# First feed-forward product of half batches 2.1, 3.0 and 3.1 in groups of four by seven block products

## The chip, the cores and the metric

The kernel runs on one core of one Trainium2 chip. The metric is device time in microseconds (us) of one execution, the median of several. A core has TensorE (PE in the profile, with its weight loads as PEld), VectorE (DVE), ScalarE (ACT), GpSimd (Pool) and SyncE (SP), each with its own queue of instructions that it works through in order; an instruction waits until what it reads has been written and what it overwrites has been read. Data lie in SBUF, and PE writes its products into PSUM.

## The reference

Attention in which a query sees only the keys of its own cluster, followed by a feed-forward layer:

```python
q_assign = np.argmax(np.einsum('bhsd,hcd->bhsc', q_n, c_n), axis=-1)
k_assign = np.argmax(np.einsum('bhsd,hcd->bhsc', k_n, c_n), axis=-1)
mask = q_assign[:, :, :, None] == k_assign[:, :, None, :]
scores = np.where(mask, scale * np.matmul(q, k.transpose(0, 1, 3, 2)), -1000000000.0)
attn = softmax(scores);  attn_out = np.matmul(attn, v)
...
x = attn_out.transpose(0, 2, 1, 3).reshape(B * S, H * D)
h = x @ w_in
g = h * (1.0 / (1.0 + np.exp(-h)))
out = g @ w_out
```

There are 4 batches, 8 heads, 768 positions of 64 features and 16 clusters. x is 3072 x 512, w_in 512 x 2048, w_out 2048 x 512; all arrays are float32, and the kernel multiplies in 16 bits (f16).

## The kernel before, in words

**Attention.** Each of the 32 pairs of batch and head is a job. Its q and k rows are normalised, split and transposed into a 128-row operand `ab`, whose lower rows are codes of the cluster, so that one product gives masked scores. A word `s.N` (L344) makes two score matmuls of 384 columns into PSUM, `x.N` (L349) is the exp on ACT that turns them into `P` (a pool of 14 buffers), `pv` (L361, 36 matmuls of 65 columns) multiplies by v with a column of ones, `nm` (L371 and L373 on DVE) divides by that column's sum, and `xd`/`xp` transpose the result into `xts[b, c]`, the operand x of the feed-forward layer. Code rows come about by `L` and `ls` (L179 on DVE), `mx` (L195), `ge` (L204), `sc` (L211 and L212 on Pool), `cx` (L220, a transposing DMA on SP) and `mv` (L224, a DMA from Pool or SP). `vc` (L285) is a cast of v on Pool.

**First product.** A half batch b.c (c is 0 or 1) has 384 tokens. Its hidden features are 16 blocks of 128. A unit `au.b.c.f` (L409) makes one block: four matmuls, one for each 128 rows of w_in, of 384 columns. The silu is kept as tanh and gating: with the weights halved beforehand, `t.b.c.f` (L429, ACT) takes the tanh out of PSUM, and `g.b.c.f` (L432, DVE) computes (tanh + 1) times h, with the tanh from SBUF and h from PSUM, into `gt`. A double unit `a2` makes two blocks in one pair of banks, with one tanh (L454) and one gate (L455) of 768 columns. A half batch so takes 64 matmuls of 384 columns.

**Second product.** For batch 0 it is plain (`b`, L467). From batch 1 on, `Pair` takes 128-token pieces two at a time by seven block products in place of eight: `ps` are sums of gated activations on DVE (L535, 128x1024 in f16), `pp` is a product of eight matmuls of 256 columns (L554), and `p1`, `pa`, `pu`, `pc`, `pd` put the results together on ACT and DVE (L560 to L586); `pf` and `pe` store them. `tw` (L500) are sums of w_out.

**Order.** All of this is one list of words, `order`, from L685 on; the program goes through it once, and each engine's queue holds its instructions in the order of the words. Attention of later batches is interleaved with the feed-forward layer of earlier ones, so that PE has work while ACT takes the exps. The words of the last third begin with score word `s.152`; at that place the attention of the last jobs (24 to 31), the rest of batch 2's first product and the second product of batches 1 and 2 lie beside each other.

Of the kernel before, what the change touches and what calls it, by code (L numbers as in the profile page):

```python
# [34 lines left out]
def kernel(  # L35
# [33 lines left out]
    def bank(name, dtype=f32, n=None):  # L69
        return ps.tile([128, 512 if dtype is f32 else 1024], dtype, name=name, tag=f"b{n}", bufs=1)  # L70
# [388 lines left out]

    pos = {}  # L460
# [217 lines left out]
    def stk_ev(pst1):  # L678
# [11 lines left out]
        hi.6.A hi.x0.P mx.4 L.3.16@1 v.6.S ge.4 ev.7.q.A lo.6 v.7.S cd.4 x.1 s.2 L.5.16@2 ce.4.D x.2 ev.7.k.D  # L690
        od.0 cg.4 s.3 tr.6.kq@03 mx.3 x.3 hi.x1.P ld.8 ge.3 s.4 ev.6.k.D x.4 ev.6.q.D s.5 mx.5 L.6.16@1 ge.5 x.5
        s.6 mx.6 cd.5 w.3 ct.3@03 x.6 ge.6 lo.x0 cd.6 vc.2 s.7 cq.3 s.8 w.0 x.7 ce.5.D tr.x0.k@0 ck.3 vc.5 cg.5
        L.7.32@2 ce.6.A vc.3 ls.7 pv.0.0.0.x@3 x.8 cg.6 s.9 vc.6 mx.7 tr.x0.q@1 x.9 w.1 ge.7 s.10 ev.x0.q.D cd.7
        vc.7 pv.0.0.1.x x.10 ev.x0.k.D s.11 w.2 lo.x1 pv.0.0.2.x ce.7.A w.5 L.x0.32.0.6@1 x.11 L.x0.32.6.12 cg.7
        s.12 w.9 ls.x0 w.7 pv.2.0.0.x@0 x.12 s.13 mx.x0 w.6 pv.2.0.1.x x.13 ge.x0 w.4 pv.2.0.2.x nm.0.0 cd.x0
        s.14 w.8 ce.x0.A tr.x1.k@2 x.14 s.15 cg.x0 ev.x1.k.D x.15 s.16 tr.x1.q@3 x.16 L.x1.32.0.6@1 s.17
        ev.x1.q.D x.17 L.x1.32.6.12 s.18 ls.x1 pv.4.0.0.x@2 x.18 nm.2.0 s.19 pv.4.0.1.x x.19 mx.x1 s.20 xp.2.0@3
        pv.4.0.2.x ge.x1 x.20 xe.2.0.D xp.0.0@0 s.21 nm.4.0 s.22 x.21 pv.6.0.y.0@3 xe.0.0.D x.22 xp.4.0@2 s.23
        xe.4.0.D ab.0.0.7@0 hi.8.D x.23 w.10.22 cd.x1 s.24 pv.6.0.y.1 x.24 w.11.23 s.25 nm.6.0 ab.0.0.6@2 x.25
        s.26 ce.x1.D xp.6.0@3 x.26 cg.x1 s.27 xe.6.0.D ab.0.0.0@1 ld.9 x.27 ae.0.0.7 ae.0.0.0 ae.0.0.6  # L700
        ab.0.0.4@3 t.0.0.0 ld.10 t.0.0.7 ae.0.0.4 g.0.0.0 s.28 t.0.0.6 s.29 g.0.0.7 x.28 ab.0.0.1@1 g.0.0.6
        ae.0.0.1 x.29 ab.0.0.2@0 ae.0.0.2 s.30 t.0.0.1 s.31 t.0.0.2 g.0.0.1 ab.0.0.3@2 t.0.0.4 ae.0.0.3
        ab.0.0.5@1 g.0.0.4 t.0.0.3 g.0.0.2 ae.0.0.5 au.0.0.8@3 t.0.0.5 g.0.0.3 x.30 au.0.0.10@0 g.0.0.5 t.0.0.8
        au.0.0.9@2 g.0.0.8 au.0.0.11@1 t.0.0.9 t.0.0.10 s.32 g.0.0.9 x.31 pv.0.1@3 g.0.0.10 hi.9.D t.0.0.11 s.33
        x.32 g.0.0.11 au.0.0.12@2 nm.0.1 x.33 au.0.0.13@0 lo.9 t.0.0.12 s.34 t.0.0.13 s.35 g.0.0.12 x.34
        au.0.0.14@1 tp.9 lo.8 xp.0.1@3 b.0.0.1.0@2 xe.0.1.A g.0.0.13 x.35 b.0.0.0.0@3 t.0.0.14 ld.11 s.36
        g.0.0.14 pv.2.1@0 x.36 hi.10.D tp.8 lo.10 s.37 au.0.0.15@1 b.0.0.0.1 t.0.0.15 x.37 v.8.S g.0.0.15 s.38
        ld.12 nm.2.1 b.0.0.0.2 x.38 v.9.S s.39 hi.11.A b.0.0.1.1 tp.10 x.39 lo.11 b.0.0.1.2 vc.8 s.40 L.9.32@1
        x.40 s.41 tp.11 L.8.32@0 x.41 b.0.0.0.3 ls.8 vc.9 mx.8 pv.4.1@0 be.0.0.0.A ls.9 mx.9 xp.2.1@3 s.42 ge.8
        s.43 xe.2.1.D x.42 v.10.S ge.9 cd.8@1 b.0.0.2.0@3 ce.8.D v.11.S x.43 hi.12.D cg.8 s.44 nm.4.1 b.0.0.2.1  # L710
        ld.13 x.44 lo.12 s.45 cd.9@1 xp.4.1@0 b.0.0.2.2 ce.9.D tp.12 xe.4.1.A x.45 L.10.32@1 s.46 ls.10
        L.11.32@0 x.46 s.47 ls.11 b.0.0.1.3 cg.9 x.47 mx.10 ld.14 ge.10 s.48 mx.11 s.49 x.48 cd.10@1 pv.6.1@0
        ge.11 v.12.S hi.13.D ce.10.A v.13.S x.49 cg.10 b.0.0.2.3 nm.6.1 be.0.0.1.A s.50 lo.13 bs.0.0.1 cd.11@1
        L.12.32@0 ce.11.A xp.6.1@2 s.51 ls.12 tp.13 xe.6.1.A au.0.1.1@1 be.0.0.2.D x.50 au.0.1.0@0 mx.12 x.51
        s.52 au.0.1.3@2 t.0.1.0 vc.13 t.0.1.1 g.0.1.0 ld.15 au.0.1.2@3 x.52 vc.10 ge.12 g.0.1.1 s.53 vc.11
        t.0.1.2 cg.11 au.0.1.5@0 hi.14.D t.0.1.3 od.1 ld.16 g.0.1.2 x.53 au.0.1.4@1 od.2 lo.14 vc.12 s.54 v.14.S
        t.0.1.4 pv.8.0@3 t.0.1.5 x.54 g.0.1.4 tp.14 s.55 g.0.1.5 cd.12@1 g.0.1.3 ce.12.A L.13.32@0 x.55 s.56
        ls.13 au.0.1.6@1 mx.13 au.0.1.7@2 cg.12 t.0.1.6 nm.8.0 vc.14 bs.0.0.2 au.0.1.8@0 t.0.1.7 g.0.1.6 v.15.S
        au.0.1.9@3 g.0.1.7 t.0.1.8 v.16.S ge.13 au.0.1.11@1 hi.15.D t.0.1.9 x.56 ld.17 au.0.1.10@2 g.0.1.9
        g.0.1.8 s.57 t.0.1.10 cd.13@3 s.58 x.57 ce.13.D au.0.1.12@0 g.0.1.10 cg.13 t.0.1.11 au.0.1.15@3 lo.15  # L720
        t.0.1.12 v.17.S x.58 au.0.1.13@2 vc.15 g.0.1.12 tp.15 s.59 g.0.1.11 t.0.1.13 L.14.32@0 x.59 s.60 ls.14
        au.0.1.14@1 mx.14 b.0.1.0.0@0 t.0.1.14 ge.14 v.18.S t.0.1.15 g.0.1.14 s.61 v.19.S hi.16.A g.0.1.15
        b.0.1.0.1 ld.18 g.0.1.13 x.60 cd.14@1 pv.10.0@3 v.20.S x.61 ce.14.A b.0.1.1.0@2 nm.10.0 cg.14 vc.19 s.62
# [220 lines left out]
```

## Time and profile before

| | us |
|---|---|
| median of three runs | 297.63 (297.48 to 298.21) |
| the profiled execution's span, first to last instruction | 295.4 |
| PE busy | 287.9 (97%) |
| DVE busy | 217.7 (74%) |
| ACT busy | 227.5 (77%) |
| Pool busy | 58.3 (20%) |
| first matmul of s.152 | 202.43 |
| exps, L349, 192 of them | 149.9 |
| first product, L409, 512 matmuls of 384 columns | 95.5 |
| gates of single units, L432, 110 of them | 57.8 |

The profile is of one execution; its span leaves out what lies before the first and behind the last instruction, and the difference to the median is 2.2 us. A row of the timeline gives the start in us from the span's start, the busy time in us, engine, line of the program, operation, output and inputs by the program's names, shape and count, and in brackets how long the engine stood idle before it and on what. Instructions on PE are pipelined, so that the busy times of neighbours overlap; what one costs is the distance from its start to the next one's. In the windows each engine has its busy time with the number of instructions, and the columns behind are TensorE's granted clock, the share of DMA and GB/s.

### The profile page before, as it was taken

What the parts mean: (1) busy time and instruction counts of PE and PEld (TensorE: products, weight loads), DVE (VectorE), ACT (ScalarE), POOL (GpSimd) and SP (SyncE); (2) the same over time, 40 slices, a digit from 0 to 9 for tenths busy, and PEclk for the clock granted to TensorE, in tenths of its full rate; (3) what the DMA queues carried; (4) which work ended last, traced back from release to release, by engine and by line L of the source; (5) the groups of instructions that cost most, each with busy time, mean ns of one, the idle gap of its engine ahead of it and who ended that gap; (6) DMA issues with size and microseconds to landing.
All of it is one profiled execution on the core that took longest, in us unless ns stands there. A gap on an engine that the chain in (4) does not pass through costs nothing.

```text
span 295.4 us, 8176 instructions
## 1 busy us (share of the span) xinstructions
PE 287.9 (97%) x3297; PEld 206.3 (70%) x3297; DVE 217.7 (74%) x458; ACT 227.5 (77%) x376; POOL 58.3 (20%) x116
## 2 busy tenths in 40 slices
PE   7799999999999999999999999999999999999995
PEld 3677666567666566678777778676777777777784
DVE  5899648677897998999578779957544563568582
ACT  4999999767987779898898988878688787464321
POOL 2489310020311102233401202542000000000000
PEclk9999999999999999999999999999999999999999
DMA  6978999998999979898689699984320210211023
GB/s 206 298 213 123 178 214 200 218 213 206 244 215 251 175 166 248 171 192 182 151 158 256 138 171 253 154 147 128 88 75 3 45 46 2 54 57 60 2 107 107
DMA packets 80548, 45.13 MB, mean 153 GB/s; under 512 B 58368, under 2 KB 77120, under 8 KB 80512
## 3 DMA queue, kind: packets, MB, share of 16 engines
q1 hardware_dynamic: 76080, 38.39, 57.2%
q0 software_dynamic: 4000, 5.82, 11.0%
q8 instruction: 25, 0.41, 0.6%
q10 hardware_dynamic: 432, 0.43, 0.4%
q14 instruction: 11, 0.09, 0.1%
HBM read 27.30 MB, written 6.29 MB: 114 GB/s over the span
## 4 chain that ended last, share of the span: by engine, by line
PE 89%; DMA 6%; DVE 3%; ACT 1%; SPq 0%; issue 0%; ACTq 0%
PE ph L409 28%; PE pS L344 19%; PE po L554 19%; PE pO L361 11%; PE po L467 7%; PE psN L167 3%; DMA ab<-cd 3%; DMA vn<-in_v_dram 2%; DMA raw<-in_q_dram 1%; DVE hl L120 1%; DVE ab L154 1%; PE junk L622 0%; DVE om L204 0%; DVE mxn L195 0%; PE px L382 0%; PE pTk L143 0%
## 5 line engine op out<-in xcount | busy, mean ns | idle before, releaser
L349 ACT ACTIVATE P<-pS 128x768 f16<-128x768 f32 x192 | 149.9, 815 | 22.8 <-PE pS L344 21.2
L409 PE MATMUL ph<-xt,win_s 128*128 128x384 f16 x512 | 95.5, 326 | 0.0
L344 PE MATMUL pS<-ab 128*128 128x384 f16 x384 | 86.0, 326 | 0.5 <-ACT P L349 0.2
L432 DVE SCALAR_TENSOR_TENSOR gt<-tn,ph 128x384 f16<-128x384 f32 x110 | 57.8, 550 | 35.9 <-ACT tn L429 35.5
L409 PEld LDWEIGHTS <-win_s 128*128 128x128 f16 x512 | 49.3, 98 | 30.2
L429 ACT ACTIVATE tn<-ph 128x384 f32<-128x384 f32 x110 | 51.0, 497 | 14.2 <-PE ph L409 13.3
L344 PEld LDWEIGHTS <-ab 128*128 128x128 f16 x384 | 34.4, 98 | 18.0 <-issue 0.9
L361 PEld LDWEIGHTS <-P 128*128 128x128 f16 x1152 | 39.8, 97 | 4.3 <-DVE ab L269 0.3
L361 PE MATMUL pO<-vt,P 128*128 128x65 f16 x1152 | 41.3, 193 | 0.2 <-DVE ab L269 0.2
L285 POOL CAST vt<-vn 128x384 f16<-128x384 f32 x32 | 18.7, 599 | 91.6 <-DMA vn<-in_v_dram 73.0
L554 PEld LDWEIGHTS <-gt 128*128 128x128 f16 x328 | 31.7, 98 | 6.6 <-DVE gt L535 0.2
L120 DVE SCALAR_TENSOR_TENSOR hl<-raw,hl 128x768 f16<-128x768 f32 (+3 forms) x35 | 31.8, 916 | 2.0 <-ACT hl L111 1.8
L554 PE MATMUL po<-wout_s,gt 128*128 128x256 f16 x216 | 28.0, 273 | 0.0
L467 PE MATMUL po<-wout_s,gt 128*128 128x512 f16 x96 | 24.0, 379 | 0.0
L167 PEld LDWEIGHTS <-ab 128*128 128x128 f16 x458 | 16.9, 97 | 3.9 <-DVE ab L154 0.8
L373 DVE TENSOR_TENSOR xn<-pO,zr 128x384 f16<-128x384 f32 x32 | 17.8, 558 | 1.1
L167 PE MATMUL psN<-stk,ab 128*128 128x32 f16 (+1 forms) x458 | 18.5, 188 | 0.2 <-DVE ab L154 0.2
L179 DVE TENSOR_REDUCE L<-psN 128x192 f32<-128x384 f32 (+1 forms) x27 | 14.9, 552 | 5.0 <-PE psN L167 4.7
L211 POOL TENSOR_SCALAR od<-od 128x96 f16<-128x96 f16 x16 | 8.0, 499 | 50.4 <-DVE od L204 50.4
L554 PE MATMUL po<-tw,sg 128*128 128x256 f16 x144 | 17.5, 273 | 0.0
L554 PEld LDWEIGHTS <-sg 128*128 128x128 f16 x144 | 14.1, 98 | 2.5
L467 PEld LDWEIGHTS <-gt 128*128 128x128 f16 x96 | 8.9, 98 | 8.2
(101 smaller groups left out, 252.1 us busy)
## 6 DMA issues: line engine op xcount, KB each, us to landing
raw<-in_k_dram SPq DMA_DIRECT2D x31, 192.0 KB, 3.8
out_dram<-ot SPq DMA_DIRECT2D x23, 256.0 KB, 2.5
vn<-in_v_dram SPq DMA_DIRECT2D x27, 192.0 KB, 3.7
raw<-in_q_dram SPq DMA_DIRECT2D x24, 192.0 KB, 3.4
win_s<-in_moe_w_in_dram POOLq DMA_DIRECT2D x8, 256.0 KB, 7.1
wout_s<-in_moe_w_out_dram POOLq DMA_DIRECT2D x4, 512.0 KB, 13.8
cp<-gt SPq DMA_DIRECT2D x4, 256.0 KB, 3.2
vn<-in_v_dram POOLq DMA_DIRECT2D x5, 192.0 KB, 3.6
```

The lines of the kernel that those rows point to most:

```text
L120: nc.vector.scalar_tensor_tensor(out=hl[:, s, 1, :], in0=raws[job.name][:, s, :], scalar=QS, in1=hl[:, s, 0, :], op0=ALU.mult, op1=ALU.sub ...
L167: nc.tensor.matmul(L[:, n % g, :, n // g], ab[:, i, :], stk[:, job.groups[i // 3][0], x : x + w], start=(x == 0), stop=(x + w == 2 * HC),)
L285: nc.gpsimd.tensor_copy(vt[:, :, 0:D], vns.pop(i))
L344: nc.tensor.matmul(pS[:, e, 0:HALF], abs_[kj.name][:, kn, :], rhs, start=True, stop=True)
L349: nc.scalar.activation(out=P, in_=pst.pop(u)[:, :, 0:HALF], func=AF.Exp, bias=0.0, scale=ESC)
L361: nc.tensor.matmul(o[:, (2 * t + h) * VW : (2 * t + h + 1) * VW], Ps[i + h, c, j // 2][:, j % 2, ts(t, 128)], vtb[(i + h) % 13][:, j, 0:VW ...
L373: nc.vector.tensor_tensor(out=xn, in0=ov[:, :, 0:D], in1=zr.unsqueeze(2).to_broadcast([128, 2 * NM, D]), op=ALU.mult)
L409: nc.tensor.matmul(ph[:, 0:HALF], win_s[:, r, ts(fb, 128)], xts[b, c][:, r, :], start=(r == 0), stop=(r == NR - 1))
L429: nc.scalar.activation(out=tn, in_=ph[:, 0:HALF], func=AF.Tanh, bias=0.0, scale=1.0)
L432: nc.vector.scalar_tensor_tensor(out=gt[:, fb, :], in0=tn, scalar=1.0, in1=ph[:, 0:HALF], op0=ALU.add, op1=ALU.mult)
L467: nc.tensor.matmul(po, gts[b, c][:, fc, ts(t, 128)], wout_s[:, fc, :], start=(fc == 0), stop=(fc == NFB - 1))
L554: nc.tensor.matmul(o, l[:, f, :], x, start=(f == 0 and k in begins), stop=(f == HK - 1), skip_group_check=True)
```

## The change

For half batches 2.1, 3.0 and 3.1 (48 of 128 feature blocks in all) the units are replaced by groups. A group `q.b.c.s`, s from 0 to 3, makes four feature blocks, 2s and 2s+1 of the lower eight and of the upper eight, for all 384 tokens. It sees w_in's part as 2 x 2 blocks (rows 0 to 255 and 256 to 511; lower and upper features) and x as 2 x 2 blocks (the same rows; tokens 0 to 191 and 192 to 383), and forms the product by seven block products in place of eight. A block product `q.b.c.s.k` is four matmuls of 192 columns (L539), so a group has 28 of them where units had 16 matmuls of 384.

The block products need sums: `un.n.s` (L482) are sums of w_in, `ws`, 128x512 in f16, 16 in all, which all three half batches use; `tt.b.c.n` (L494) are sums of x, 128x384, four for each half batch. Of the 16 sums of w_in 12 go to Pool and 4 to DVE, of the 12 of x 9 to Pool and 3 to DVE. Behind the products, three results of a group are copied out of PSUM into `cc` in float32 (`qc`, 24 on ACT, L549, and 12 on DVE, L551), and three sums on DVE (`qa`, L556) add a PSUM bank to a `cc`. Four tanh (`qt`, L563) and four gates (`qg`, L576) of 384 columns follow; for three of the four quarters h lies in `cc`, in SBUF, for the fourth in PSUM. `cc` comes from the same pool of 14 buffers as `P`. The nine double units of these half batches are gone with the single ones.

The list is another one from `s.152` on, the exps and scores of the last jobs come in another order among themselves, and unit au.2.0.14 stands behind s.152. The loads and stores on SP change places a little. The lines of the second product move by 121 (L535 is L656 after).

On Pool, from the last `mv.27` (L224 with ab_3682) on, the old order has, with `od` the code rows, `vt` the cast v and `uu` a zeroed buffer:

```order
L211 TENSOR_SCALAR od_508<-od_508 128x2x16x3
L212 TENSOR_SCALAR od_508<-od_508 128x2x16x3
L285 CAST vt3_73<-vn_4188 128x6x64
L504 MEMSET uu_4400 128x256
L224 DMA ab_3973<-cdt_4354 16x6x256
L285 CAST vt5_75<-vn_4599 128x6x64
```

and the new one, with `ws` the sums of w_in and `tt` those of x:

```order
L482 TENSOR_TENSOR ws_4348<-win_s_66 128x512
L482 TENSOR_TENSOR ws_4348<-ws_4348,win_s_66 128x512
L482 TENSOR_TENSOR ws_4393<-win_s_66,ws_4348 128x512
L482 TENSOR_TENSOR ws_4348<-win_s_66 128x512
L482 TENSOR_TENSOR ws_4393<-win_s_66 128x512
L211 TENSOR_SCALAR od_508<-od_508 128x2x16x3
L212 TENSOR_SCALAR od_508<-od_508 128x2x16x3
L494 TENSOR_TENSOR tt_4440<-xt_4009 128x384
L224 DMA ab_3973<-cdt_4406 16x6x256
L482 TENSOR_TENSOR ws_4476<-win_s_66,ws_4393 128x512
L494 TENSOR_TENSOR tt_4440<-xt_4009,tt_4346 128x384
L482 TENSOR_TENSOR ws_4476<-win_s_66 128x512
```

Five sums of w_in now stand ahead of the code rows of the last job but one, and more sums around the DMA that carries them.

On DVE, from the reduction `L` of the code rows beside s.152 on, the old order has:

```order
L179 TENSOR_REDUCE L_4345<-psN_4321 128x192
L195 TENSOR_REDUCE mxn_4356<-L_4345 128x12
L204 TENSOR_TENSOR od_508<-L_4345,mxn_4356 128x2x96
L432 SCALAR_TENSOR_TENSOR gt_3641<-tn_4343,ph_4338 128x384
L432 SCALAR_TENSOR_TENSOR gt_3641<-tn_4270,ph_4265 128x384
L432 SCALAR_TENSOR_TENSOR gt_3641<-tn_4365,ph_4360 128x384
L535 TENSOR_TENSOR sg_4402<-gt_3641 128x1024
L535 TENSOR_TENSOR sg_4414<-sg_4402,gt_3641 128x1024
```

The new one, up to the first sum `sg` for the second product:

```order
L494 TENSOR_TENSOR tt_4346<-xt_4009,tt_4346 128x384
L556 TENSOR_TENSOR cc_4383<-qb_4395,cc_4383 128x384
L551 COPY cc_4417<-qb_4412 128x384
L551 COPY cc_4424<-qa_4419 128x384
L482 TENSOR_TENSOR ws_4393<-ws_4393,win_s_66 128x512
L556 TENSOR_TENSOR cc_4424<-qb_4442,cc_4424 128x384
L556 TENSOR_TENSOR cc_4432<-qb_4412,cc_4432 128x384
L576 SCALAR_TENSOR_TENSOR gt_4377<-tn_4409,cc_4383 128x2x192
L656 TENSOR_TENSOR sg_4469<-gt_3641 128x1024
L482 TENSOR_TENSOR ws_4476<-win_s_66 128x512
L656 TENSOR_TENSOR sg_4491<-sg_4469,gt_3641 128x1024
```

What is shown here stands behind the same three gates; the two sums `sg` were next behind them, and now seven copies, sums and a gate stand in between, and a weight sum between the two.

The diff, cut to its core:

```diff
+    def w_sum(n, s, eng):
...
+        o = wsums[n, s] = hosts[tag][:, at]
...
+        x, y, op = {
+            1: (a21, a22, ALU.add), 2: (wsums.get((1, s)), a11, ALU.subtract),
+            3: (a11, a21, ALU.subtract), 4: (a12, wsums.get((2, s)), ALU.subtract),
+        }[n]
+        eng.tensor_tensor(out=o, in0=x, in1=y, op=op)
+    def x_sum(b, c, n, eng):
...
+        eng.tensor_tensor(out=o, in0=p, in1=y, op=op)
+    class Quad:
...
+        def product(self, k, bk):
...
+            for g in range(2):
+                f = 2 * s + g
+                for r in range(2):
...
+                    nc.tensor.matmul(
+                        o[:, g * QT : (g + 1) * QT], w, y,
+                        start=(k in (1, 2, 5) and g == 0 and r == 0), stop=(r == 1), skip_group_check=True,
+                    )
+        def copy(self, k, eng):
+            n = {1: 0, 2: 1, 5: 2}[k]
+            self.cc[n] = mp.tile([128, HALF], f32, name="cc", tag="P", bufs=NP)
+            i = (self.G if k == 5 else self.A)[:, 0:HALF]
+            if eng == "A":
+                nc.scalar.activation(out=self.cc[n], in_=i, func=AF.Copy, bias=0.0, scale=1.0)
+            else:
+                nc.vector.tensor_copy(self.cc[n], i)
+        def add(self, k):
+            n = {1: 0, 2: 2, 3: 1}[k]
+            i = (self.B if k == 1 else self.A if k == 2 else self.G)[:, 0:HALF]
+            nc.vector.tensor_tensor(out=self.cc[n], in0=i, in1=self.cc[n], op=ALU.add)
+        def src(self, n):
+            return self.A[:, 0:HALF] if n == 3 else self.cc[n]
+        def tanh(self, n):
+            t = self.tn[n] = mp.tile([128, HALF], f32, name="tn", bufs=4)
+            nc.scalar.activation(out=t, in_=self.src(n), func=AF.Tanh, bias=0.0, scale=1.0)
...
+        def gate(self, n, eng):
...
+            eng.scalar_tensor_tensor(
+                out=self.gt[:, f : f + 2, h], in0=self.tn[n].rearrange("p (g n) -> p g n", g=2), scalar=1.0,
+                in1=self.src(n).rearrange("p (g n) -> p g n", g=2), op0=ALU.add, op1=ALU.mult,
+            )
...
+        x.151 pe.1.1.x L.29.32@0 nm.24.0 pe.1.1.p ls.29 s.152 x.152 tt.2.1.1.D un.1.0.P v.31.S mx.29 g.2.0.13 ge.29
```

More of the change, by code (lines that the diff above doesn't have):

```diff
@@ L458, in unit_a2, with wsum @@
         return act
+    HF, QT = NFB // 2, HALF // 2
+    HOSTS = (("raw7", 3), ("hl0", 3), ("hl1", 3), ("ab0", 3), ("ab1", 3), ("cp0", 2))
+    hosts, wsums, tts, quads = {}, {}, {}, {}
+    def wsum(n, s):
+        return wsums[n, s]
+    def w_sum(n, s, eng):
+        at = 4 * s + n - 1
+        for tag, room in HOSTS:
+            if at < room:
+                break
+            at -= room
+        if tag not in hosts:
+            hosts[tag] = mp.tile([128, room, 2, 256], f16, name="ws", tag=tag, bufs=1)
+        o = wsums[n, s] = hosts[tag][:, at]
+        lo_, up = slice(256 * s, 256 * s + 256), slice(DF // 2 + 256 * s, DF // 2 + 256 * s + 256)
+        a11, a12, a21, a22 = win_s[:, 0:2, lo_], win_s[:, 2:4, lo_], win_s[:, 0:2, up], win_s[:, 2:4, up]
+        x, y, op = {
[3 more added lines that the diff above has]
+        eng.tensor_tensor(out=o, in0=x, in1=y, op=op)
@@ new lines, in x_sum @@
+    def x_sum(b, c, n, eng):
+        x = xts[b, c]
+        b11, b12, b21, b22 = x[:, 0:2, 0:QT], x[:, 0:2, QT:HALF], x[:, 2:4, 0:QT], x[:, 2:4, QT:HALF]
+        if n in (1, 3):
+            tts[b, c, n] = mp.tile([128, 2, 2, QT], f16, name="tt", tag="vn", bufs=5)
+        o = tts[b, c, n - 1 + n % 2][:, (n + 1) % 2]
+        p, y, op = {
+            1: (b12, b11, ALU.subtract), 2: (b22, n == 2 and tts[b, c, 1][:, 0], ALU.subtract),
+            3: (b22, b12, ALU.subtract), 4: (b21, n == 4 and tts[b, c, 1][:, 1], ALU.subtract),
+        }[n]
+        eng.tensor_tensor(out=o, in0=p, in1=y, op=op)
@@ L690 @@
[L690 to L699, printed above, removed]
@@ L815, in unit, with quad @@
         return tuple(int(y) for y in x[:3])
+    def quad(x):
+        if unit(x) not in quads:
+            quads[unit(x)] = Quad(*unit(x))
+        return quads[unit(x)]
     def pair(x):
@@ L898 @@
         "pp": lambda x, k: pair(x).product(int(x[3]), k),
+        "q": lambda x, k: quad(x).product(int(x[3]), k),
+        "qc": lambda x, k: quad(x).copy(int(x[3]), x[4]),
+        "qa": lambda x, k: quad(x).add(int(x[3])),
+        "qt": lambda x, k: quad(x).tanh(int(x[3])),
+        "qg": lambda x, k: quad(x).gate(int(x[3]), Pl if x[4:] and x[4] == "P" else V),
+        "qz": lambda x, k: quad(x).silu(int(x[3])),
+        "al": lambda x, k: nc.scalar.preload_act_table(AF.Silu),
+        "un": lambda x, k: w_sum(int(x[0]), int(x[1]), Pl if x[2:] and x[2] == "P" else V),
+        "tt": lambda x, k: x_sum(int(x[0]), int(x[1]), int(x[2]), Pl if x[3:] and x[3] == "P" else V),
         "p1": lambda x, k: pair(x).p1(),
```

279 lines of the change are left out of this document (172 added, 107 removed).

## The prediction

> **What bounds the kernel now.** I read the page's head and its chain of waits first, then the windows from the point at which the list changes, then the timelines of PE, DVE, ACT and Pool there.
>
> ```profile
> span 295.4 us, 8176 instructions
> PE 287.9 (97%) x3297; PEld 206.3 (70%) x3297; DVE 217.7 (74%) x458; ACT 227.5 (77%) x376; POOL 58.3 (20%) x116
> ...
> PE 89%; DMA 6%; DVE 3%; ACT 1%; SPq 0%; issue 0%; ACTq 0%
> ```
>
> The chain that ended last is PE's. The windows (PE, PE's weight loads, DVE, ACT, Pool, granted clock, DMA) show that it waits for nothing in the last third:
>
> ```profile
> 200.00:210.00 10.00, 10.00 (x108) 7.11 (x106) 6.89 (x14) 8.24 (x17) 1.96 (x5) 1.00 0.55 144
> ...
> 202.00:292.00 90.00, 90.00 (x871) 67.79 (x869) 55.06 (x103) 55.81 (x94) 2.46 (x6) 1.00 0.19 57
> ...
> 290.00:295.40 5.40, 2.05 (x18) 1.49 (x16) 1.16 (x4) 0.38 (x1) 0.00 (x0) 1.00 0.28 100
> ```
>
> The clock is 1.00 throughout, DVE and ACT are busy 61 to 62%, and Pool is all but idle. The new list starts with s.152:
>
> ```profile
> 202.43 0.81 PE L344 MATMUL pS<-ab 128*128 128x384 f16 x4
> ...
> 291.67 0.38 PE L554 MATMUL po<-zz,gt 128*128 128x256 f16 x2
> ```
>
> So PE runs 89.6 us without a gap from there to 292.05, and whatever PE is spared or made to wait there is the change of the whole. The profiled span is 295.4 against a median of 297.63: 2.2 us lie around it, which I carry over unchanged. About 0.3% (0.9 us) is what a measurement of this kernel can tell from no change.
>
> **PE: fewer columns.** Busy times overlap, so I price by the distance from one start to the next.
>
> ```profile
> 253.97 1.26 PE L361 MATMUL pO<-vt,P 128*128 128x65 f16 x36
> ...
> 255.07 0.81 PE L409 MATMUL ph<-xt,win_s 128*128 128x384 f16 x4
> ...
> 257.24 0.33 PE L382 MATMUL px<-ident,xn 128*128 128x128 f16 x3
> 257.41 1.46 PE L409 MATMUL ph<-xt,win_s 128*128 128x384 f16 x8
> ...
> 258.71 1.04 PE L554 MATMUL po<-wout_s,gt 128*128 128x256 f16 x8
> ...
> 259.58 2.76 PE L409 MATMUL ph<-xt,win_s 128*128 128x384 f16 x16
> ```
>
> 384 columns: 1.30/8 = 162.5 ns. 256: 0.87/8 = 109 ns. 128: 0.17/3 = 57 ns. 65: 1.10/36 = 31 ns. A 192-column matmul, which the trace doesn't have, lies between the 128 and 256 rows: midway, 83 ns. A group replaces 16 x 162.5 ns = 2.60 us by 28 x 82.5 ns = 2.31 us; twelve groups spare 12 x 0.29 = **3.5 us**. Bounds: at 57 ns it would be 12.0 us, at 109 ns a loss of 5.4; since four sizes lie on one line I keep to 3 to 4.
>
> The Trainium skill (TensorE: Matmul & The Clock Gate, Back-to-back issue gap) gives 81 ns as the sustained spacing at 128 columns, limited by the weight loads; by it 192 columns would take an estimated 89 ns, the sum spare 1.3 us in place of 3.5, and the forecast be 301.5. The rows above, 57 ns at 128 columns and 31 at 65, speak against it, and I leave the sum at 3.5.
>
> **DVE and ACT: more to do.** Per group come three copies out of PSUM (24 of the 36 on ACT), three sums on DVE, and four tanh and four gates of 128x384; nine double tanh and gates become single ones. Prices, start to start:
>
> ```profile
> 197.84 0.56 DVE L373 TENSOR_TENSOR xn<-pO,zr 128x384 f16<-128x384 f32 x1
> 198.31 0.54 DVE L432 SCALAR_TENSOR_TENSOR gt<-tn,ph 128x384 f16<-128x384 f32 x1
> ...
> 202.34 0.55 DVE L179 TENSOR_REDUCE L<-psN 128x192 f32<-128x384 f32 x1
> 202.92 0.50 DVE L195 TENSOR_REDUCE mxn<-L 128x12 f32<-128x192 f32 x1
> ...
> 203.78 1.71 DVE L432 SCALAR_TENSOR_TENSOR gt<-tn,ph 128x384 f16<-128x384 f32 x3
> ...
> 285.35 0.68 DVE L535 TENSOR_TENSOR gt<-gt,sg 128x1024 f16<-128x1024 f16 x1
> 285.95 0.68 DVE L535 TENSOR_TENSOR gt<-gt 128x1024 f16<-128x1024 f16 x1
> ```
> ```profile
> L500 DVE TENSOR_TENSOR zz<-wout_s,tw 128x512 f16<-128x512 f16 x1 | 0.4, 419 | 0.0
> ```
> ```profile
> 202.63 0.49 ACT L429 ACTIVATE tn<-ph 128x384 f32<-128x384 f32 x1 [1.06 <-PE ph L409]
> 203.02 1.51 ACT L349 ACTIVATE P<-pS 128x768 f16<-128x768 f32 x2
> 204.40 0.51 ACT L429 ACTIVATE tn<-ph 128x384 f32<-128x384 f32 x1
> ```
>
> DVE: 0.47 for a gate of 384 columns, and I take it for a copy or sum of that size too; 0.60 for an f16 sum of 1024; 0.42 busy less the same overlap of 0.08, so 0.34, for one of 512, and 0.30 for 384. ACT: tanh 0.39, exp 0.69, copy as tanh. Added on DVE: 48 copies and sums x 0.47 = 22.6, the double gates' second start about 0.6, seven sums of w_in and x about 2.3: some 25 us, so DVE goes from 55 to 80 of about 87. On ACT: 24 copies x 0.39 = 9.4 and nine more starts, 10 in all, so 66. Neither is over PE in all; what counts is the stretch.
>
> *Start stretch.* From s.152 up to product 6 of pair 2.0.p PE has eight score words of two 384-column matmuls (0.325), two units of four (0.65), twelve block products (four of 192 columns, 0.33) and one second product (eight of 256, 0.87): 2.6 + 1.3 + 4.0 + 0.87 = 8.7 us. That product needs the second of the two sums sg; on DVE stand seventeen rows up to it: nine gates, sums and copies x 0.47 = 4.2, two sg x 0.60, two weight sums x 0.34, two x sums x 0.30, and L195 and L204, 202.92 to the next gate at 203.78 in the old profile, 0.9: 7.6 us. DVE starts them at 202.9, where L195 starts above; PE starts at about 201.8, since unit au.2.0.14 (0.65) now comes behind s.152. So 7.6 + 1.1 = 8.7 against 8.7: nothing to spare. ACT, at 8.24 of 10 already in the window from 200, gets the copies as well. I put **+0.5** for this (0 to 1.2).
>
> *End stretch.* From product 3 of group 2 of 3.0 to product 5 of pair 3.1.p PE has 37 block products x 0.33, fourteen second products x 0.87 and a transpose, 24.6 us; DVE has 24 gates and 17 sums x 0.47, seven sums x 0.60, two of 512 f32 columns x about 0.6 and two of 256 x about 0.34, 25.2 us, and behind that the delays to its first start and from its last sum. Here DVE is the bound by a little: **+1.0** (0 to 2.0).
>
> **Pool's sums hold DVE.** Twelve weight sums of 128x512 and nine x sums of 128x384 go to Pool, which stood idle:
>
> ```profile
> 197.61 0.56 POOL L224 DMA_DIRECT2D ab<-cdt  x1
> 203.96 0.48 POOL L211 TENSOR_SCALAR od<-od 128x96 f16<-128x96 f16 x1 [5.79 <-DVE od L204]
> ```
> ```profile
> L285 POOL CAST vt<-vn x32: 494/510/1317, 11.6 to 220.4; 128x384 f16<-128x384 f32 x32
> ```
>
> No two-input sum of size runs on Pool in this trace. A cast of 384 takes 510 ns, 1.3 ns an element: 0.7 us for 512 if both inputs are read at once, 1.4 if in turn; I take 1.05. The Trainium skill (GPSIMD Engine Reference, Elementwise — side-by-side cycle accounting) has about 2.6 cycles an element for a two-input sum, an estimated 1.1 us; no row shows it.
>
> What Pool does is not free for DVE. Three places (the last names the usual times):
>
> ```profile
> 98.73 0.55 DVE L115 TENSOR_SCALAR hl<-raw 128x768 f16<-128x768 f32 x1
> 98.81 0.84 POOL L285 CAST vt<-vn 128x384 f16<-128x384 f32 x1 [3.73 <-DMA vn<-in_v_dram]
> ...
> 99.20 1.26 DVE L120 SCALAR_TENSOR_TENSOR hl<-raw,hl 128x768 f16<-128x768 f32 x1
> ```
> ```profile
> 179.64 0.68 DVE L535 TENSOR_TENSOR sg<-sg,gt 128x1024 f16<-128x1024 f16 x1
> 180.24 0.75 DVE L535 TENSOR_TENSOR gt<-gt 128x1024 f16<-128x1024 f16 x1
> ```
> ```profile
> 179.78 0.71 POOL L212 TENSOR_SCALAR od<-od 128x96 f16<-128x96 f16 x1
> ```
> ```profile
> L120 DVE SCALAR_TENSOR_TENSOR hl<-raw,hl x35: 359/951/1256, 4.0 to 188.1; 128x768 f16<-128x768 f32 x26, 128x576 f16<-128x576 f32 x7, 128x384 f16<-128x384 f32 x1, 128x192 f16<-128x192 f32 x1
> ```
> ```profile
> L212 POOL TENSOR_SCALAR od<-od x16: 288/291/708, 112.4 to 204.4; 128x96 f16<-128x96 f16 x16
> ```
>
> The cast took 0.84 in place of 0.51, beside L115; L120, which reads two operands in SBUF and was next, then took 1.26 in place of 0.95. L212 took 0.71 in place of 0.29 beside sums of DVE, and the second of those 0.75 in place of 0.68. One engine waits for the other.
>
> ```profile
> L432 DVE SCALAR_TENSOR_TENSOR gt<-tn,ph x110: 535/548/556, 40.8 to 282.2; 128x384 f16<-128x384 f32 x110
> ```
>
> The old gates, with one operand in PSUM, never spread. Three of four new gates take both operands from SBUF, and so do the weight, x and sg sums. The Trainium skill (SBUF — State Buffer, SBUF: two separate sides) states that DVE with two SBUF inputs and a Pool operation that reads SBUF exclude each other for a whole instruction; the rows agree (0.31 us and 0.42 us of waiting).
>
> The first five weight sums run from 198.2, before DVE's new work. The next eight Pool sums fall, by the order and these prices, in the first 16 us, in which DVE has sixteen operations with two SBUF inputs. One Pool sum makes at most one of them wait, for half its time on average: seven waits x 0.53 = **+3.7 us** (bounds: nothing, and eight whole sums, 8 x 1.05 = 8.4). With a stretch that has nothing to spare they come out at PE in full. DVE's weight sums and x sums are behind them too, and PE's block products behind those.
>
> The sum: -3.5 + 0.5 + 1.0 + 3.7 = +1.7 on the profiled span, so **299.3 us**.
>
> **The rivals.** *Pool's sums cost nothing (other side).* If DVE's waits fall where it waits for a tanh or a product anyway, or if Pool's sums are done before DVE's new gates come, the sum is -3.5 + 0.5 + 1.0 = -2.0: 295.6. For it: in the window 202 to 292 DVE was idle 39% of the time, and five sums run early. Against it: those 39% are filled in this stretch. It decides at 1.1 us of DVE held in the first 16 us: below that the kernel is faster by over 0.9. *Short waits.* If each lasts 0.31, as behind the cast, 7 x 0.31 = 2.2: +0.2, 297.8, no change to be seen. For it: the only row with a wait on DVE's side is of that size. Against it: the sum is twice a cast. *Weight loads set PE's pace.*
>
> ```profile
> L409 PEld LDWEIGHTS <-win_s 128*128 128x128 f16 x512 | 49.3, 98 | 30.2
> ```
>
> If a 192-column matmul can't start more often than the 98 ns of a load, a group takes 2.74 us and PE loses 1.7 where it should gain 3.5: 299.3 + 5.2 = 304.5. Against it stand the 57 and 31 ns above. That the change doesn't do what it says is out: the new order has 336 block matmuls of 192 columns.
>
> **How the numbers follow.** Held by Pool, 299.3: 0.38, its own range 298.5 to 302.0 (sums of 1.4 us, 7 x 0.70 = 4.9, an end stretch of 2.0 and 0.5 for the last x sums, which fall into it: +4.4). Free of it, 295.6: 0.36. Short waits, 297.8: 0.20. Weight loads: 0.06. The range takes in the first three: 295.2 (the free case with an end stretch of 0.6 for 1.0) to 302.0; 8.4 for Pool's sums would need every one to hold DVE from its first moment, and stays out with the weight loads. Faster 0.36, same 0.20, slower 0.44.
>
> **What would show it.** In the changed profile: L539 at 83 ns start to start (right) or 98 (loads); Pool's L482 at about 1.05 us; gates of L576 with a maximum far over 0.55 us between 203 and 219 beside a Pool sum; PE below 10.00 in the windows from 200 to 220 and 265 to 290, and full between. If L576 never spreads and PE stays full, the term of 3.7 is wrong and 295.6 right.

## The result and the profile after

The changed kernel takes 308.0 us where the one before takes 297.8: slower, ratio 1.0343 (95% interval 1.0315 to 1.0372). A second set of runs on another occasion gave 307.92 against 297.87, ratio 1.0321 (1.0283 to 1.0358). The forecast of 299.3 and its range up to 302.0 are missed. The execution that was profiled first was a longer one at a lower clock (span 311.4, clock 0.989), so the lines here are from a second profile of the same kernel, span 306.2, where nothing else is said; here and below, such executions are left out of the times.

```profile
span 306.2 us, 8632 instructions
PE 288.6 (94%) x3441; PEld 214.9 (70%) x3441; DVE 249.7 (82%) x522; ACT 238.2 (78%) x409; POOL 81.9 (27%) x137
...
PE 67%; DVE 12%; DMA 8%; ACT 8%; issue 3%; SPq 1%; DVEq 0%; ACTq 0%
```

DVE, ACT and "issue" now hold 23% of the chain that ended last, where they held 4%. The windows (PE, weight loads, DVE, ACT, Pool, clock, DMA) show where PE stands still: in 200 to 220 and from 260 on, and hardly in between.

```profile
200.00:210.00 10.00, 9.52 (x117) 7.29 (x116) 8.24 (x18) 8.89 (x17) 8.07 (x10) 1.00 0.45 122
210.00:220.00 10.00, 6.75 (x80) 4.81 (x78) 9.85 (x13) 5.98 (x12) 10.00 (x10) 1.00 0.03 7
...
230.00:240.00 10.00, 10.00 (x121) 8.68 (x120) 8.30 (x18) 8.34 (x16) 1.78 (x2) 1.00 0.31 74
...
270.00:280.00 10.00, 8.59 (x86) 7.63 (x87) 8.05 (x17) 5.50 (x14) 0.00 (x0) 1.00 0.07 25
280.00:290.00 10.00, 8.31 (x83) 7.26 (x81) 7.68 (x16) 5.41 (x15) 0.00 (x0) 1.00 0.08 29
```

PE's busy time understates this, since each stop lets the last matmul's tail count as busy. So I went through the starts of all matmuls from 195 us on and took from each distance to the next start that matmul's own price (163, 109, 82.5, 57 or 30 ns by its columns). What is left is called PE's loss below. Before it is 0.2 us up to 230 and 0.1 from 260 on; now it is **6.2 us up to 230, 0.3 from 230 to 260 and 7.2 from 260 on**.

*The price of 192 columns* is as forecast (three rows of the first profile's PE timeline): 0.33 us for four, 82.5 ns each.

```profile
256.64 0.49 PE L539 MATMUL qa<-tt,win_s 128*128 128x192 f16 x4
256.97 0.49 PE L539 MATMUL qa<-tt,ws 128*128 128x192 f16 x4
257.30 0.49 PE L344 MATMUL pS<-ab 128*128 128x384 f16 x2
```

So PE's own work did fall by 3.5 us, and -3.5 + 6.0 + 0.3 + 7.1 = +9.9 is the measured +10.1. (The two profiled spans differ by 10.8; 0.9 of it lies ahead of the new list already, where the reduction L179 starts at 203.21 in place of 202.34.)

*The start.* DVE's timeline, where the sums and gates with two operands in SBUF stretch, and Pool's beside it:

```profile
209.56 0.56 DVE L556 TENSOR_TENSOR cc<-qb,cc 128x384 f32<-128x384 f32 x1 [0.23 <-issue]
210.03 0.55 DVE L576 SCALAR_TENSOR_TENSOR gt<-tn,cc 128x384 f16<-128x384 f32 x1
210.50 1.40 DVE L656 TENSOR_TENSOR sg<-gt 128x1024 f16<-128x1024 f16 x1
211.82 1.37 DVE L482 TENSOR_TENSOR ws<-win_s 128x512 f16<-128x512 f16 x1
213.11 1.64 DVE L656 TENSOR_TENSOR sg<-sg,gt 128x1024 f16<-128x1024 f16 x1
214.67 1.50 DVE L576 SCALAR_TENSOR_TENSOR gt<-tn,cc 128x384 f16<-128x384 f32 x1
216.10 0.55 DVE L556 TENSOR_TENSOR cc<-qa,cc 128x384 f32<-128x384 f32 x1
```
```profile
208.94 1.16 POOL L482 TENSOR_TENSOR ws<-win_s,ws 128x512 f16<-128x512 f16 x1
210.05 1.30 POOL L494 TENSOR_TENSOR tt<-xt,tt 128x384 f16<-128x384 f16 x1
211.31 2.89 POOL L482 TENSOR_TENSOR ws<-win_s 128x512 f16<-128x512 f16 x2
214.16 3.02 POOL L482 TENSOR_TENSOR ws<-ws,win_s 128x512 f16<-128x512 f16 x2
```

The sums sg take 1.40 and 1.64 in place of 0.68, the weight sum 1.37 in place of 0.41, a gate 1.50 in place of 0.55; the adds L556, with one operand in PSUM, keep their 0.55. Each waits for about one Pool sum, and Pool's sums stretch as well, from 1.16 to between 1.33 and 1.60. The Trainium skill (SBUF — State Buffer, SBUF: two separate sides) states the exclusion of such pairs; these rows agree.

PE waits for what DVE so makes late. From 200 to 230 no wait of PE or DVE is for a Pool sum itself, so it is not that these come too late. Two rows of PE's waits from 195 to 230 (us in total, times, longest):

```profile
PE qa L539 <- DVE ws L482: 1.4, 1, 1.4
PE po L675 <- DVE sg L656: 0.7, 1, 0.7
```

*The end.* Two rows of PE's waits from 260 to 300, and one group of DVE's lines there (busy and mean ns; then the idle time before it):

```profile
PE qq L539 <- ACT cc L549: 1.9, 5, 0.6
PE qq L539 <- DVE cc L556: 1.9, 2, 1.2
```
```profile
L556 DVE TENSOR_TENSOR cc<-qq,cc 128x384 f32<-128x384 f32 x12 | 6.7, 554 | 4.0 <-PE qq L539 2.1 <-ACT tn L563 1.1 <-ACT cc L549 0.7
```

PE waits for copies and sums that take a product out of PSUM, and DVE stands idle for 4 us ahead of these same sums, half of it for PE's product and half for ACT. One round, whole (all engines, 285 to 287):

```profile
285.38 0.49 PE L539 MATMUL qq<-xt,ws 128*128 128x192 f16 x4
...
285.92 0.49 ACT L549 ACTIVATE cc<-qq 128x384 f32<-128x384 f32 x1 [2.54 <-PE qq L539]
...
286.44 0.56 DVE L556 TENSOR_TENSOR cc<-qq,cc 128x384 f32<-128x384 f32 x1 [0.69 <-ACT cc L549]
...
287.05 0.49 PE L539 MATMUL qq<-tt,ws 128*128 128x192 f16 x4 [1.17 <-DVE cc L556]
```

Product, copy, sum, next product: 1.67 us from start to start, of which PE works 0.33. This is the longest of twelve stops ahead of products of 3.1, which cost 0.1 to 1.3 us each and 5.9 of the 7.2 us together.

What PE waits for there is mostly not the bank that it writes. A group of 3.1 takes a pair of banks as one tile, `qq`. The product at 287.05 goes into the first bank, which the copy has read by 286.41; it starts 0.05 us after the end of the sum, which reads the second bank. At eleven of the twelve stops the product starts 0.05 to 0.06 us after the end of a read of the other bank of its pair. In 2.1 and 3.0 each bank is a tile of its own: there a product follows, in the list, a read of another bank of its group 105 times, and 26 times it starts before that read has ended. In 3.1 it does so at none of 42. (The timelines give the times, and the order of the words gives the bank of each row.) This points to the pair being one tile as what makes copies, sums and products take turns. No run here had two tiles in its place, so this is read from the trace alone, and what two tiles would bring back is not shown.

### The profile page after: what moved, and what is told of

It reads as the page before. It is cut to its first block, busy times and chain, and to the rows that moved or that the text cites. A ratio compares the mean times of both kernels' runs of the same rounds, so it can differ in the third digit from the quotient of the medians.

```text
span 311.4 us, 8632 instructions
## 1 busy us (share of the span) xinstructions
PE 288.8 (93%) x3441; PEld 215.7 (69%) x3441; DVE 253.8 (82%) x522; ACT 238.0 (76%) x409; POOL 79.1 (25%) x137
## 4 chain that ended last, share of the span: by engine, by line
PE 74%; DVE 10%; ACT 7%; DMA 4%; issue 2%; SPq 1%; DVEq 0%; ACTq 0%
PE pS L344 18%; PE ph L409 16%; PE po L675 14%; PE pO L361 11%; PE po L588 6%; DVE gt L576 5%; PE psN L167 3%; PE qa L539 2%; ACT P L349 2%; PE qb L539 2%; PE qq L539 2%; DMA vn<-in_v_dram 2%; ACT cc L549 2%; DMA ab<-cd 1%; DVE cc L556 1%
## 5 line engine op out<-in xcount | busy, mean ns | idle before, releaser
L409 PE MATMUL ph<-xt,win_s 128*128 128x384 f16 x320 | 59.9, 326 | 0.0
L432 DVE SCALAR_TENSOR_TENSOR gt<-tn,ph 128x384 f16<-128x384 f32 x80 | 41.8, 549 | 17.0 <-ACT tn L429 16.8
L409 PEld LDWEIGHTS <-win_s 128*128 128x128 f16 x320 | 30.7, 98 | 19.6 <-DVE xn L373 0.3
L429 ACT ACTIVATE tn<-ph 128x384 f32<-128x384 f32 x80 | 37.1, 500 | 5.5 <-PE ph L409 4.6
L675 PEld LDWEIGHTS <-gt 128*128 128x128 f16 x328 | 31.5, 98 | 5.1 <-DVE gt L576 0.3
L576 DVE SCALAR_TENSOR_TENSOR gt<-tn,cc 128x384 f16<-128x384 f32 x36 | 28.5, 809 | 1.5 <-ACT tn L563 1.3
L539 PEld LDWEIGHTS <-ws 128*128 128x128 f16 x192 | 16.8, 99 | 15.2 <-DVE ws L482 8.6
L563 ACT ACTIVATE tn<-cc 128x384 f32<-128x384 f32 x36 | 17.8, 522 | 3.1 <-DVE cc L556 2.2
L179 DVE TENSOR_REDUCE L<-psN 128x192 f32<-128x384 f32 (+1 forms) x27 | 14.9, 551 | 5.7 <-PE psN L167 5.4
L675 PE MATMUL po<-tw,sg 128*128 128x256 f16 x144 | 18.7, 281 | 0.6 <-DVE sg L656 0.6
```

The lines of the kernel that those rows point to most:

```text
L409: nc.tensor.matmul(ph[:, 0:HALF], win_s[:, r, ts(fb, 128)], xts[b, c][:, r, :], start=(r == 0), stop=(r == NR - 1))
L429: nc.scalar.activation(out=tn, in_=ph[:, 0:HALF], func=AF.Tanh, bias=0.0, scale=1.0)
L432: nc.vector.scalar_tensor_tensor(out=gt[:, fb, :], in0=tn, scalar=1.0, in1=ph[:, 0:HALF], op0=ALU.add, op1=ALU.mult)
L539: nc.tensor.matmul(o[:, g * QT : (g + 1) * QT], w, y, start=(k in (1, 2, 5) and g == 0 and r == 0), stop=(r == 1), skip_group_check=True,)
L576: eng.scalar_tensor_tensor(out=self.gt[:, f : f + 2, h], in0=self.tn[n].rearrange("p (g n) -> p g n", g=2), scalar=1.0, in1=self.src(n).re ...
L675: nc.tensor.matmul(o, l[:, f, :], x, start=(f == 0 and k in begins), stop=(f == HK - 1), skip_group_check=True)
```

## The experiments

Two theories were kept apart for each stretch. Start: DVE is held by Pool's sums (as forecast), or the stretch is over-full without Pool. End: handoffs (PE waits for a bank of PSUM to be read before it may write it again), or DVE is full. The first four runs also asked whether DVE is held for one sum or for a whole run of them, since the first profile had shown a gate of 9.07 us. "us" is the median, with the ratio to the kernel before by its interval; the losses are PE's, as above, of the one profiled run of each (that of gates_twice took 318.4). They hold what PE lost by matmuls at a lower granted clock, too: up to 230 about 1.3 us in sums_gap, 1.4 in sums_dve and 2.3 in sums_earlier, from 260 on 1.6 in units_31 and 4 in gates_twice.

| kernel | us | ratio | up to 230 | 230 to 260 | from 260 |
|---|---|---|---|---|---|
| again | 307.9 | 1.028 to 1.036 | 6.2 | 0.3 | 7.2 |
| sums_gap | 307.9 | 1.028 to 1.038 | 6.2 | 0.3 | 7.2 |
| sums_dve | 312.6 | 1.039 to 1.052 | 7.5 | 2.7 | 8.9 |
| before_pool8 | 298.4 | 0.998 to 1.004 | 0.2 | 0 | 0.1 |
| sums_earlier | 311.4 | 1.040 to 1.050 | 9.0 | 0.8 | 7.2 |
| copies_still | 306.2 | 1.024 to 1.031 | – | – | – |
| gates_twice | 316.0 | 1.058 to 1.067 | 6.1 | 0.3 | 17.9 |
| units_31 | 308.1 | 1.029 to 1.041 | 6.1 | 0.4 | 7.4 |
| sums_memset | 303.5 | 1.015 to 1.021 | 2.2 | 0.3 | 6.8 |
| both_still | 303.3 (two runs) | – | 6.1 | 0.3 | 2.4 |
| memset_still | 297.8 | 0.998 to 1.002 | 2.1 | 0.3 | 0.9 |
| units_31b | 311.2 (one run) | – | – | – | – |

**again**, no edit:

> The changed kernel once more, for a second profile. Theory (whole run): one DVE gate with both operands in SBUF (L576) again lasts as long as Pool's run of sums behind it, 7 to 9 us, and PE stands idle for about that long around 210 to 220; 308 us. Rival (one at a time): the 9.07 us gate was an accident of one execution; no L576 lasts over 1.8 us in this one.

No gate lasted over 1.50 us here, and the time was 307.9. So the rival holds in this execution, and the kernel is slow without 9 us of one gate.

**sums_gap**

```diff
         eng.tensor_tensor(out=o, in0=x, in1=y, op=op)
+        if eng is nc.gpsimd:
+            nc.gpsimd.memset(gap, 0.0)
```

> The changed kernel with a memset of one element per partition on Pool behind each of its 21 sums, so that no two of them follow each other directly. Theory (whole run): if an instruction that reads nothing ends Pool's run, DVE gets in after each sum, no L576 lasts over 1.8 us, and the time is 299 to 303; if it doesn't end the run, the gate lasts as long as before or a little longer, and the time stays at 308 to 310. Rival (one at a time): the 9 us have another cause and stay: 308.

Nothing moved: losses of the same size, same instructions stretched. Separating Pool's sums by something short doesn't help here, as each is waited for singly already.

**sums_dve**

```diff
-        "un": lambda x, k: w_sum(int(x[0]), int(x[1]), Pl if x[2:] and x[2] == "P" else V),
+        "un": lambda x, k: w_sum(int(x[0]), int(x[1]), V),
```

and the same for the sums of x.

> All 21 of Pool's sums of w_in and x are made by DVE instead, at the same places of the list. Theory (whole run): the 9 us gate is gone, PE's 8.2 us of idle time with it; DVE gets 12 x 0.34 + 9 x 0.30 = 6.8 us more, of which the first stretch, which has nothing to spare, pays 2 to 4: 302 to 304 us. Rival (one at a time): the gate waited for something else, and DVE with 6.8 us more is only slower: 308 to 313.

312.6 us lies in the rival's range, near its upper end. The first stretch pays 7.5 us in place of 6.2, but 1.4 of it went to matmuls at a lower clock (0.66 in the window from 210 to 215), so the fourteen of the sums that fall there cost PE about as much on DVE as Pool's holding did; later an x sum, now in DVE's queue, makes it stand for x's transposing DMA, with other sums behind it, and PE loses 2.1 of the 2.7:

```profile
247.38 0.36 DVE L494 TENSOR_TENSOR tt<-xt 128x384 f16<-128x384 f16 x1 [2.47 <-DMA xt<-xn]
```

**before_pool8**

```diff
+            nc.gpsimd.tensor_tensor(out=ws, in0=win_s[:, 0:2, 0:256], in1=win_s[:, 2:4, 0:256], op=ALU.add)
```

eight times, in a tile that nobody reads, in the kernel before.

> The kernel before with eight more sums of w_in on Pool in one run behind mv.30, whose results nobody reads. Theory (whole run): the next sum for the second product on DVE (L535, two operands in SBUF) that comes after the run has begun, at about 211.7, lasts until the run ends at about 215.5, so some 4 us in place of 0.68; PE waits for part of it: 299 to 302. Rival (one at a time): no L535 lasts over 1.9 us there, and the time is 297.6 to 298.3.

No change. Pool's eight sums took 10.95 us together, and of the sums L535 of DVE (L540 here) that fall beside them none took over 0.84:

```profile
208.34 10.95 POOL L463 TENSOR_TENSOR ws<-win_s 128x512 f16<-128x512 f16 x8
```
```profile
214.64 0.84 DVE L540 TENSOR_TENSOR sg<-cp 128x1024 f16<-128x1024 f16 x1
```

Only three such sums of DVE fall there, the gates have an operand in PSUM, and DVE has idle time: here Pool's sums were free. It is the new kernel's stretch that pays for them.

**sums_earlier**: all 16 words `un` on Pool, one each behind s.139 to x.156, their room in another order:

```diff
-    HOSTS = (("raw7", 3), ("hl0", 3), ("hl1", 3), ("ab0", 3), ("ab1", 3), ("cp0", 2))
+    HOSTS = (("raw7", 3), ("hl1", 3), ("hl0", 3), ("ab0", 3), ("ab1", 3), ("cp0", 2))
```

> All 16 sums of w_in on Pool, but made from s.139 on, as soon as their room is free, mostly one at a time and nearly all of them ahead of the new gates. Theory (Pool holds DVE, one sum at a time): DVE's long instructions between 209 and 222 are gone, of the 6.2 us that PE lost between 200 and 230 some 4 come back, and the time is 303 to 305. Rival (the stretch is over-full even without Pool): PE loses 5 to 6 us there all the same, 306 to 308; should the code rows, which share Pool's queue, come late, it is slower than 308.

The case named last came: the DMA that carries code rows stood behind the sums in Pool's queue, and PE waited 4.2 us for it. So it tells nothing of the two theories, only that Pool's queue had no room there.

```profile
PE pS L344 <- DMA ab<-cdt: 4.2, 1, 4.2
```

**copies_still**

```diff
+            if getattr(self, "two", None) is not None:
+                i = win_s[:, 0, 0:HALF]
```

> In the four groups of 3.1 the copies on ACT read an operand in SBUF instead of the product in PSUM, so that ACT does as much, but the next block product into that bank needn't wait for it (the sums that follow are of other values). Theory (handoffs: at the end PE waits for a copy or a sum before it may write the same bank again): of the 7.2 us that PE lost between 260 and 300 some 3 to 5 come back, 303 to 305. Rival (DVE is full there): nothing comes back but 0 to 1, 307 to 308.

306.0 to 306.4 us: 1.7 us came back, less than the handoff theory asked and more than the rival. The copies are a part only; that PE then still waits for the sums is likely, but not shown, since its profile is of a run of 374.9 us.

**gates_twice**: each gate of 3.1 issued twice.

> Each of the 16 gates of 3.1 on DVE is made twice, 16 x 0.47 = 7.5 us more DVE work in the end stretch, with nothing else changed. Rival (DVE is full there): the kernel gets 6 to 8 us slower, 314 to 316. Theory (handoffs): DVE has idle time between them that takes up half or more of it, 309 to 312.

8.1 us slower, by this test a point for the rival. But DVE's idle time ahead of the twelve sums is the same 4.0 us as without the extra gates, which a full engine wouldn't have:

```profile
L556 DVE TENSOR_TENSOR cc<-qq,cc 128x384 f32<-128x384 f32 x12 | 6.6, 554 | 4.0 <-PE qq L539 1.5 <-ACT cc L549 1.3 <-ACT tn L563 1.2
```

Nor are the 8.1 us the price of the gates alone. In the profiled run some 4 of the 17.9 us are matmuls at a lower clock (0.64 to 0.68 in the windows from 285 to 295), and the clock of the other three runs was 0.989 to 0.995; and PE stood 3.5 us for gates ahead of the second product. That gates ahead of a sum lengthen the round as well is likely, but this run does not single it out.

**units_31**: words q, qc, qa and tt of 3.1 out, each q.3.1.s.1 and q.3.1.s.4 two plain units in the pair of banks.

> Half batch 3.1 alone goes back to plain units (two feature blocks at a time in the pair of banks, single tanh and gates at the places of the new list, no copies, no sums, no x sums); 2.1 and 3.0 stay in groups. PE gets 4 x 0.29 = 1.2 us more work. Theory (handoffs): PE's 7.2 us lost between 260 and 300 fall to 2 to 3, 303 to 305. Rival (DVE is full there): DVE is spared 16 sums and copies or so, 5 to 6 us of work, and the gain is of the same size, but then the kernel with the gates made twice is slower by all of its 7.5.

No clear change (its interval and that of the kernel again overlap); neither range came. It has a wait of its own: PE stood 2.0 us for the late gates of the first two units, and ran at half its pace for 2.4 us behind it. **units_31b** was to mend that:

> Half batch 3.1 in plain units as before, with each tanh directly behind its products and the gates a few words on, so that the wait of 2 us for late tanh and gates that the first such kernel had is gone. Theory (handoffs): PE's loss from 260 on falls from 7.2 to about 3, PE has 1.2 us more work, 304 to 305.5. Rival (DVE is full there with the sums of 3.0 and of the second product): the loss stays at 5 or more, 306 to 308.

Its time of 311.2 is above both ranges, and its profile is of a run of 317.6, so it decides nothing. What plain units in 3.1 alone would be worth stays open; a list made for them wasn't tried.

**sums_memset**

```diff
+        if eng is nc.gpsimd:
+            nc.gpsimd.memset(o, 0.0)
+        else:
+            eng.tensor_tensor(out=o, in0=x, in1=y, op=op)
```

> Pool's 21 sums are replaced by memsets of the same tiles (of other values; they read nothing and take about 0.3 to 0.6 us). DVE does what it did. Theory (DVE waits for Pool's sums because both read SBUF): no DVE sum or gate lasts over 0.8 us between 200 and 225, PE's loss there falls from 6.2 to 0.5 to 2 us, and the time is 303 to 304. Rival (the stretch is over-full with DVE's own work): PE still loses 4 to 6 us there, 306 to 307.5.

As the theory had it: the loss up to 230 falls from 6.2 to 2.2 us, a little more than the 2 that were expected at most, and the time by 4.4. The same DVE instructions beside Pool's memsets (DVE's timeline, and Pool's casts):

```profile
211.16 0.68 DVE L662 TENSOR_TENSOR sg<-gt 128x1024 f16<-128x1024 f16 x1
211.77 0.42 DVE L485 TENSOR_TENSOR ws<-win_s 128x512 f16<-128x512 f16 x1
212.10 0.68 DVE L662 TENSOR_TENSOR sg<-sg,gt 128x1024 f16<-128x1024 f16 x1
212.71 1.49 DVE L582 SCALAR_TENSOR_TENSOR gt<-tn,cc 128x384 f16<-128x384 f32 x1
```
```profile
212.81 0.97 POOL L285 CAST vt<-vn 128x384 f16<-128x384 f32 x2
```

Only the gate that meets Pool's casts, which read SBUF, is still held, against the expectation of none over 0.8.

**both_still**: as copies_still, and in `add` too:

```diff
             i = (self.B if k == 1 else self.A if k == 2 else self.G)[:, 0:HALF]
+            if getattr(self, "two", None) is not None:
+                i = win_s[:, 0, 0:HALF]
```

> In the four groups of 3.1 the copies on ACT and the sums on DVE read an operand in SBUF in place of the product in PSUM (other values), so that both engines do as much as before, but PE needn't wait for them before the next block product into the same bank. Theory (handoffs): of the 7.2 us lost from 260 on at least 5 come back, 302 to 303.5. Rival (DVE is full there): as its work is the same, 0 to 2 come back, 306 to 308.

303.3 us: 4.7 of the 7.2 came back, with DVE's work the same 6.7 us for the twelve sums and its idle time ahead of them gone. So DVE's work by itself accounts for no more than the 2.4 us that are left. The edit takes away every read of the pair by a copy or a sum, so it does not tell a wait for the same bank from one for the other.

```profile
L560 DVE TENSOR_TENSOR cc<-win_s,cc 128x384 f32<-128x384 f16 x12 | 6.7, 566 | 0.0
```

**memset_still**: sums_memset and both_still together.

> Both together: memsets for Pool's sums, and no handoffs in 3.1 (other values). If the two losses are all that stands between the prediction's 3.5 us saved and the measured time, this one comes to 295 to 298; if a third cause is left, 300 or more.

297.8 us, ratio 0.9997 (0.9976 to 1.0018). With Pool's holding and the handoffs of 3.1 out, the losses are 2.1 + 0.3 + 0.9 = 3.3 us, and the 3.5 that PE is spared pay for just these. Gain and losses close, so no third cause of size is left outside them, and no version here beats the kernel before. In its windows from 260 to 280 PE (first column) and DVE (third) are both busy throughout, so DVE's work does fit beside PE's, with nothing to spare:

```profile
260.00:270.00 10.00, 10.00 (x113) 9.54 (x111) 10.00 (x21) 7.79 (x20) 0.00 (x0) 1.00 0.07 22
270.00:280.00 10.00, 10.00 (x107) 9.39 (x105) 10.00 (x22) 7.68 (x20) 0.00 (x0) 1.00 0.15 54
```

## Why the prediction was wrong

- **PE, -3.5.** Right: 82.5 ns for 192 columns, 3.5 us less work.
- **Start stretch, +0.5 (0 to 1.2).** Right as far as it went, and it did not go far enough. It ends at product 6 of pair 2.0.p, and up to there PE loses 0.3 us in memset_still, without Pool's sums. But 2.0 us more than before are lost up to 230; 1.7 of them lie behind product 6, where the sum has no term. The largest piece, 0.5, comes right behind the add that follows the gate held by Pool's casts, and two of 0.2 and 0.4 are scores that wait for an exp; what causes the rest is not shown.
- **Pool holds DVE, +3.7.** Right in mechanism: 6.2 - 2.2 = 4.0 us. That the size agrees so well is partly luck, since two errors cancel: DVE itself was held for longer, eight of its instructions between 206 and 221 taking 9.93 in place of 4.18 us, 5.75 more, 0.72 each where I put seven at 0.53; but PE paid some 70% of it where I put all.
- **End stretch, +1.0 (0 to 2.0).** This step failed: 7.2 us are lost. I held DVE's sum of 25.2 us (its terms add up to 25.35) against PE's 24.6 and took the difference with one delay at either end, as if the two could run side by side. The sums themselves were about right: in memset_still both engines are busy throughout. But in 3.1 a group's seven products go into one pair of banks, and a product waits until the copy or sum ahead of it has read the pair, mostly the other bank of it. The twelve stops cost PE 5.9 us, the longest round 1.67 us with 0.33 of PE's work in it. DVE in turn stands 4.0 us ahead of its sums. The forecast had no term for these turns. Taking the reads of the pair away brought back 4.7 us with Pool's sums in place, and 5.7 without them (303.5 to 297.8; by PE's losses 6.8 - 0.9 = 5.9).

The forecast's +1.7 falls short of the measured +10.1 by 8.4, 8.2 of it by these terms: 1.5 up to 230 beside Pool's share, 0.3 from Pool, 0.3 in the middle, 6.1 at the end. The forecast that it would be slower stood on Pool's holding and was right there, but only for a part of the reason: without Pool's sums the kernel would still have been slower (303.5), where the rival "Pool's sums cost nothing" had 295.6.

## What to carry to other kernels

A stretch in which engines hand one another the same tile is priced by its rounds, product to copy to sum to next product, and not only by adding up each engine's work: look for how many rounds each tile has, and what stands in the order to fill them. Look also at whether a tile spans more than what one step needs: here, with a pair of banks in one tile, products waited for reads of the other bank. Before a sum is put on an idle Pool, look at whether DVE's instructions beside it read both operands from SBUF: here that cost PE 4.0 us, while eight such sums in the kernel before, beside gates that read PSUM, cost nothing. Fewer columns on PE are only worth having where the copies and sums that they need have slack of their own.

## What the runs showed of the hardware

- In the first profile one gate was held not for one sum but for a whole run of nine Pool instructions, and PE with it; the same place showed it once more in the profile of units_31b (9.21 us). In the first profile PE's loss up to 230 was 11.2 us in place of 6.2, and its span was 5.1 us longer than the second one's. What decides between this and one sum at a time is not shown. DVE's and Pool's timelines of the first profile:

```profile
209.59 9.07 DVE L576 SCALAR_TENSOR_TENSOR gt<-tn,cc 128x384 f16<-128x384 f32 x1
218.59 0.68 DVE L656 TENSOR_TENSOR sg<-gt 128x1024 f16<-128x1024 f16 x1
```
```profile
209.79 0.92 POOL L494 TENSOR_TENSOR tt<-xt,tt 128x384 f16<-128x384 f16 x1
...
217.11 1.14 POOL L482 TENSOR_TENSOR ws<-win_s,ws 128x512 f16<-128x512 f16 x1
```

- After PE had stood still, its matmuls ran at half the pace for a while, and the granted clock in the windows fell. In units_31, after 2.03 us of standing, eight matmuls of 384 columns took 2.44 us to the next start in place of 1.30, and the clock of the window from 275 to 280 was 0.66:

```profile
274.93 2.64 PE L409 MATMUL ph<-xt,win_s 128*128 128x384 f16 x8 [2.03 <-DVE gt L621]
277.37 1.57 PE L720 MATMUL po<-wout_s,gt 128*128 128x256 f16 x8
```
```profile
275.00:280.00 5.00, 5.00 (x24) 2.92 (x24) 2.29 (x5) 0.87 (x2) 0.00 (x0) 0.66 0.00 0
```

The Trainium skill (TensorE: Matmul & The Clock Gate, What's actually happening) has the clock halved after an idle window of about 3.4 us; here 2.03 us were enough, with shorter stops in the 10 us ahead. No length of a stop decides it in these runs: in sums_gap much the same stops as in again, the longest 1.6 us, were followed by a clock of 0.67 from 215 to 220, in again by 1.00, and 1.9 us of standing in sums_dve, up to 248, by 1.00 as well.
- A Pool sum of two f16 operands took, where nothing held it, 1.14 to 1.17 us for 512 elements and 0.90 to 0.92 for 384; for 512 the forecast had taken 1.05.
